# Issuing the copy of the first batch's p on VectorE in the order of its load's arrival, and telling the planner of it

## The chip, the cores and the metric

One core of a Trainium2 chip. The metric is device time of one execution in microseconds, the median of several runs. All inputs are in HBM at the start and the output is in HBM at the end.

## The reference, cut to what matters

```python
def sm_attn(qq, kk, vv):
    s = scale * np.matmul(qq, kk.transpose(0, 1, 3, 2))
    s = s - np.max(s, axis=-1, keepdims=True)
    a = np.exp(s)
    a = a / (np.sum(a, axis=-1, keepdims=True) + 1e-09)
    return np.matmul(a, vv)
p_packed = sm_attn(p, k, v)              # p: (8, 8, 32, 64), k, v, q: (8, 8, 576, 64)
out = sm_attn(q, p_packed, p_packed)
# then, with x = out as (4608, 512):
a = x @ w1; b = x @ w2                   # 512 x 1024
h = a * b @ w3                           # 1024 x 1024
return (h @ w_out)                       # 1024 x 512
```

Eight batches of an attention in two steps (32 rows of p "pack" each batch's keys and values, then q attends to the packed rows), followed by a gated feed-forward layer.

## The kernel before

The kernel multiplies w3 by w_out once, at the start (the "fold"), so that each batch needs one product fewer. For that, w3 has to be transposed on TensorE, chunk by chunk, each chunk copied out of PSUM, where TensorE's results stand (copied to tile w3T), and then multiplied. Everything that TensorE does is put in order at build time by a greedy planner: every piece of work is a `Step` with the things that it needs, times estimated for each engine, and a rule that the step that can start first goes first. Where the planner sees an idle stretch, it puts filler matmuls on a constant tile (`keep_busy`), to hold TensorE's clock up.

```python
def load_p(b0, b1):
    nc.gpsimd.dma_start(out=pin[:, 2*b0 : 2*b1, 0, :], in_=p[b0:b1].rearrange(...))
...
load_fold(0, 1)          # w3 columns and w_out rows of fold chunk 0
load_fold(1, 2)
...
load_fold(2, 4)
load_fold(4, 6)
load_in("k", 0)
load_p(0, 1)
load_in("v", 0)
load_fold(6, 8)
load_w3(4, 6)
load_in("q", 0)
load_gate(0, 2)
load_w3(6, 8)
load_gate(2, 4)
load_gate(4, 8)
load_p(1, B)
load_in("k", 1)
load_in("v", 1)
load_in("q", 1)
nc.vector.tensor_copy(pin[:, 0:2, 1, :], pin[:, 0:2, 0, :])   # batch 0's p, a second time beside itself
nc.gpsimd.tensor_copy(pin[:, 2:, 1, :], pin[:, 2:, 0, :])     # the other batches'
...   # only now the planner emits all the steps, among them:

def emit_p(e, tags):                     # in attention(b)
    ps = one(tags, FP16)
    for g in range(2):
        nc.tensor.transpose(ps[:, 128*g : 128*g + 128], pin[:, 2*b + g, :, :]..., ident[:, :])
    ...                                  # two copies out of PSUM to pT
turned("k", "kT")                        # four steps: transposes of k, copies to kT
front.append(Step(110, emit_p, needs=[("p", b), ("packed", b - 2)], ...))
s1(0); s1(1); s1(2)                      # scores and exp
front.append(Step(862, emit_pack, needs=[("v", b, 1)] + [("es1", b, i) for i in range(3)], ...))
```

An engine executes its instructions in the order in which they were emitted. So the copy of batch 0's p stands ahead of every copy of w3T on VectorE.

The softmax here doesn't subtract the row's maximum and nothing guards it: scores larger than these inputs give would overflow.

Of the kernel before, what the change touches and what calls it, by code (L numbers as in the profile page):

```python
# [17 lines left out]
def kernel(  # L18
# [12 lines left out]
    nc = tc.nc  # L31
# [3 lines left out]
    B, H, S, D = q.shape  # L35
# [56 lines left out]
    pin = wpool.tile([128, B * 2, 2, D], FP16, name="pin")  # L92
# [20 lines left out]
    def load_in(name, b, now=0.0):  # L113
        src = {"k": k, "v": v, "q": q}[name]
        t = in_pool.tile([128, H, CK * D], FP16, name=name, tag=name)
        ins[name, b] = t
        n = 1 if b else 2
        for i in range(n):
            h0, h1 = H * i // n, H * (i + 1) // n
            nc.gpsimd.dma_start(  # L120
                out=t[0:SC, h0:h1, :],
                in_=src[b, h0:h1].rearrange("h (p c) d -> p h (c d)", c=CK),
            )
            arrives((name, b, 1), (h1 - h0) * S * D * 4, now)
            if i == 0:
                done[name, b, 0] = done[name, b, 1]
# [59 lines left out]
    load_in("k", 1)  # L186
    load_in("v", 1)
    load_in("q", 1)
    nc.vector.tensor_copy(pin[:, 0:2, 1, :], pin[:, 0:2, 0, :])
    nc.gpsimd.tensor_copy(pin[:, 2:, 1, :], pin[:, 2:, 0, :])  # L190


    F0, F1, W0, W1 = 0.30, 0.90, 2.00, 9.00
    A0, A1, A2 = -2.00, -1.40, -0.20



# [106 lines left out]
    def one_bank(b):  # L304
        if b < EARLY:
            return lambda: [(x,) for x in SINGLE + ("m2",)]
        return lambda: [("m1",), ("m3",), ("m2",)]
# [9 lines left out]
    def one(tags, dtype=FP32):  # L317
        if tags[0] == "m2":
            n = 512 if dtype == FP32 else 1024
            return psum.tile([128, 2, n], dtype, name="m2", tag="m2")[:, 0, :]  # L320
        return bank(tags[0], dtype)

    def copy(e, out, in_):
        if e == "A":
            nc.scalar.copy(out=out, in_=in_)  # L325
        else:
            nc.vector.tensor_copy(out, in_)  # L327
# [3 lines left out]
    def attention(b):  # L331
        st = state[b] = {}
        front, back = [], []
# [20 lines left out]
        def turned(name, tname):  # L354

            for hp in range(NHP):

                def emit(e, tags, hp=hp):
                    if hp == 0:
                        st[tname] = t_pool.tile([128, NHP, S], FP16, name=tname, tag=tname)  # L360
                    ps = one(tags, FP16)
                    for hc in range(6):
                        h, c3 = 2 * hp + hc // 3, hc % 3
                        nc.tensor.transpose(  # L364
                            ps[:, SC * hc : SC * hc + SC],
                            ins[name, b][0:SC, h, 128 * c3 : 128 * c3 + 128],
                            ident[0:SC, 0:SC],
                        )
                    copy(e[0], st[tname][:, hp, :], ps[:, 0:S])
                    if hp == NHP - 1 and b + 2 < B:  # L370
                        load_in(name, b + 2, now["t"])

                needs = [(name, b, hp // 2)]
                if name == "q":
                    needs.append(("scored", b - 2))
                front.append(
                    Step(
                        255,
                        emit,
                        needs=needs,  # L380
                        tags=one_bank(b),
                        post=[({"D": 455, "A": 640}, (tname, b, hp), (0,))],
                    )
                )
# [172 lines left out]
        def norm_round(g):  # L557
# [16 lines left out]
            def emit_a2(e, tags):  # L574
# [20 lines left out]
            return Step(0, emit_a2, needs=[("ri", b, g)], post=[({"D": 458}, ("a2", b, g), ())])  # L595

        turned("k", "kT")
        front.append(
            Step(
                110,  # L600
                emit_p,
                needs=[("p", b), ("packed", b - 2)],
                tags=one_bank(b),
                post=[
                    ({"D": 250, "A": 370}, ("pT", b), ()),
                    ({"D": 250, "A": 370}, ("pT", b), (0,)),
                ],
# [9 lines left out]
                needs=[("v", b, 1)] + [("es1", b, i) for i in range(3)],  # L617
                tags=one_bank(b),
                post=[({"D": 640}, ("ppn", b), (0,))],
# [4 lines left out]
        if b != 1:  # L624
# [5 lines left out]
                needs=[("ppn", b), ("grounds", b - 2)],  # L630
                tags=one_bank(b),
                post=[({"D": 260, "A": 380}, ("ppT", b), (0,))],
# [244 lines left out]
    for key in ("gated", "scored", "grounds", "packed"):  # L877
        done[key, -2] = done[key, -1] = 0.0
    att = [attention(b) for b in range(B)]
    work = [s for pair in range(B // 2) for s in project(pair)]  # L880
    run(
# [37 lines left out]
```

## Time and profile before

| | before |
|---|---|
| median of 3 runs | 237.88 us (237.17 to 238.91) |
| TensorE busy | 211.8 of 235.8 us |
| VectorE, ScalarE busy | 122.0, 139.4 us |
| TensorE's longest wait | 9.2 us, for a copy on VectorE |

In the profile, PE is TensorE's matmuls, PEld its weight loads, DVE VectorE, ACT ScalarE, POOL GpSimd. `out<-in` gives the tiles. What stands behind `<-` in brackets is what ended the idle time before the instruction, and the number before it is how long that lasted. The lines are in the prediction below.

### The profile page before, as it was taken

The page shows a single profiled execution, that of the slowest core. Times are in us where ns is not written, and L with a number is a line of the kernel's source. Part 1 is how long each engine was busy: PE and PEld are TensorE (multiplying, and loading weights), DVE is VectorE, ACT ScalarE, POOL GpSimd, SP SyncE. Part 2 cuts the span into 40 slices and gives each one's busy share as a digit, 9 for nine tenths or more (in the row PEclk, how much of TensorE's full clock was granted, in tenths as well). Part 3 has the DMA queues.
Part 4 walks back from the last instruction along what each step waited for, and adds up shares of the span by engine and source line. Part 5 has one row for each costly group of instructions (what it writes and reads, how often), then busy time and mean ns, then how long its engine had stood idle before and what let it go on. Part 6 is the DMA issues. An engine that isn't in the chain of part 4 may idle for free.

```text
span 235.8 us, 6617 instructions
## 1 busy us (share of the span) xinstructions
PE 211.8 (90%) x2736; PEld 130.6 (55%) x2767; DVE 122.0 (52%) x286; ACT 139.4 (59%) x291; POOL 36.6 (16%) x54
## 2 busy tenths in 40 slices
PE   7409899999799999998999899999999999999992
PEld 2104555457665668575666466646765545566540
DVE  1002316456572858886865594574766476444300
ACT  2000326767488688767768578776865676555421
POOL 8856440501121202111111000000000000000000
PEclk9967979999999999999999999999999999999999
DMA  7999999999999997959839422122123222332364
GB/s 78 144 198 206 198 204 198 196 204 205 170 155 186 189 201 103 197 92 170 132 81 165 83 72 47 47 72 65 46 49 90 47 79 57 89 75 65 87 156 112
DMA packets 34190, 29.52 MB, mean 125 GB/s; under 512 B 4976, under 2 KB 29040, under 8 KB 34160
## 3 DMA queue, kind: packets, MB, share of 16 engines
q0 software_dynamic: 28400, 19.66, 58.2%
q1 hardware_dynamic: 5760, 9.44, 15.3%
q8 instruction: 21, 0.34, 0.6%
q14 instruction: 9, 0.07, 0.1%
HBM read 39.32 MB, written 9.44 MB: 207 GB/s over the span
## 4 chain that ended last, share of the span: by engine, by line
PE 79%; DMA 8%; issue 3%; ACT 3%; DVE 3%; POOL 3%; DVEq 0%; ACTq 0%; POOLq 0%
PE g L673 27%; PE f L737 19%; PE m L364 7%; PE m L737 4%; DMA q<-in_q_dram 4%; PE m L483 4%; PE g L737 4%; DMA k<-in_k_dram 3%; PE m L396 3%; PE m L432 3%; DVE abT L684 2%; POOL w_sb L129 1%; PE m L797 1%; PE g L831 1%; PE m L519 1%
## 5 line engine op out<-in xcount | busy, mean ns | idle before, releaser
L673 PE MATMUL g<-a,G 128*128 128x288 f16 x512 | 87.7, 286 | 3.2 <-DVE abT L684 2.8
L684 DVE TENSOR_TENSOR abT<-g,bs 128x288 bf16<-128x288 f32 x128 | 57.7, 455 | 51.5 <-PE g L673 22.7
L673 PEld LDWEIGHTS <-G 128*128 128x128 f16 x512 | 46.2, 98 | 35.2 <-issue 11.5
L325 ACT CAST bs<-g 128x288 bf16<-128x288 f32 x128 | 50.1, 402 | 25.9 <-PE g L673 22.9
L737 PE MATMUL f<-wc_sb,abT 128*128 128x512 bf16 x186 | 55.7, 379 | 2.0 <-ACT o L325 0.3
L737 PEld LDWEIGHTS <-abT 128*128 128x128 bf16 x288 | 27.0, 98 | 15.5 <-issue 2.9
L327 DVE CAST G<-m 128x512 f16<-128x512 f32 (+1 forms) x32 | 20.1, 669 | 4.3 <-PE m L483 4.2
L325 ACT CAST G<-m 128x1024 f16<-128x1024 f32 (+1 forms) x17 | 16.4, 962 | 9.5 <-PE m L483 9.5
L325 ACT COPY kT<-m 128x576 f16<-128x576 f16 x8 | 5.2, 644 | 26.3 <-PE m L364 26.0
L737 PE MATMUL m<-wc_sb,abT 128*128 128x512 bf16 x47 | 13.4, 379 | 0.1
L403 ACT ACTIVATE es<-m 96x512 f16<-96x512 f32 x24 | 12.8, 596 | 1.1 <-PE m L396 1.1
L325 ACT COPY o<-f 128x512 f32<-128x512 f32 x18 | 10.6, 588 | 4.1 <-PE f L737 3.4
L364 PE MATMUL m<-ident,q 96*128 96x96 f16 x174 | 11.6, 206 | 1.5 <-issue 1.4
L364 PEld LDWEIGHTS <-q 96*128 96x128 f16 x192 | 10.5, 97 | 3.8 <-issue 2.0
L120 POOL DMA_DIRECT2D v<-in_v_dram x9 | 6.8, 760 | 37.1 <-PE m L432 36.4
L396 PEld LDWEIGHTS <-kT 128*96 128x96 f16 x192 | 10.6, 125 | 2.7 <-DVE pT L327 0.9
L831 PE MATMUL f<-wo_sb,w3T 128*128 128x512 f16 x8 | 3.7, 468 | 9.2 <-DVE w3T L327 9.2
L364 PE MATMUL m<-ident,k 96*128 96x96 f16 x192 | 11.7, 206 | 0.1
L364 PEld LDWEIGHTS <-k 96*128 96x128 f16 x192 | 10.4, 97 | 2.4 <-issue 0.3
L327 DVE COPY kT<-m 128x576 f16<-128x576 f16 x24 | 10.7, 451 | 1.6 <-PE m L364 1.1
L396 PE MATMUL m<-pT,kT 128*96 128x64 f16 x192 | 10.6, 208 | 1.0 <-DVE pT L327 0.7
L241 PE MATMUL m<-blk 128*128 128x512 f16 x26 | 10.0, 519 | 1.5 <-DVE blk L167 1.5
(76 smaller groups left out, 223.0 us busy)
## 6 DMA issues: line engine op xcount, KB each, us to landing
out_dram<-o SPq DMA_DIRECT2D x24, 192.0 KB, 2.4
k<-in_k_dram POOLq DMA_DIRECT2D x7, 576.0 KB, 8.8
v<-in_v_dram POOLq DMA_DIRECT2D x7, 576.0 KB, 6.7
q<-in_q_dram POOLq DMA_DIRECT2D x7, 576.0 KB, 8.5
out_dram<-o SPq DMA_DIRECT2D x24, 128.0 KB, 2.4
w_sb<-in_moe_w_dram POOLq DMA_DIRECT2D x4, 512.0 KB, 13.4
w_sb<-in_moe_w_dram POOLq DMA_DIRECT2D x7, 256.0 KB, 11.6
out_dram<-o SPq DMA_DIRECT2D x24, 64.0 KB, 2.0
```

Of the source, the lines that this page charges most:

```text
L120: nc.gpsimd.dma_start(out=t[0:SC, h0:h1, :], in_=src[b, h0:h1].rearrange("h (p c) d -> p h (c d)", c=CK),)
L241: nc.tensor.matmul(ps[:, :], blk[:, :], blk[:, :].unsqueeze(1).to_broadcast([128, 4, 128]), start=True, stop=True,)
L325: nc.scalar.copy(out=out, in_=in_)
L327: nc.vector.tensor_copy(out, in_)
L364: nc.tensor.transpose(ps[:, SC * hc : SC * hc + SC], ins[name, b][0:SC, h, 128 * c3 : 128 * c3 + 128], ident[0:SC, 0:SC],)
L396: nc.tensor.matmul(o[:, :, h % 2, h // 2, :], st["kT"][:, h // 2, c : c + SC], pT[:, h, :, :], start=True, stop=True,)
L403: nc.scalar.activation(out=st["es1"][0:SC, c3, :, :, :, :].rearrange("t e g h n -> t (e g h n)"), in_=ps[0:SC, :], func=AF.Exp, scale=scale,)
L432: nc.tensor.matmul(ps[32 * hp : 32 * hp + 32, 128 * g + d0 : 128 * g + d1], es1[0:SC, c // 2, c % 2, g, hp, :], vin[0:SC, 2 * hp + g, D * ...
L483: nc.tensor.matmul(banks[g][32 * hp : 32 * hp + 32, 0:n], ppT[64 * g : 64 * g + 64, g, 32 * hp : 32 * hp + 32], w_sb[w][64 * g : 64 * g + ...
L673: nc.tensor.matmul(ps[:, 0:HS], st["G", w][:, g, 128 * mc : 128 * mc + 128], st["a2"][:, g, half, :], start=(g == 0), stop=(g == 1),)
L684: nc.vector.tensor_mul(abT[b // 2][:, mc, b % 2, HS * half : HS * half + HS], ps[:, 0:HS], st["bs"][:, :],)
L737: nc.tensor.matmul(hold["ps"][:, :], lhsT(i), rhs(i), start=(i == 0), stop=(i == n - 1))
```

## The change

The intent: issue the copy of batch 0's p in the order in which its data arrives, so that VectorE can copy w3T chunks out of PSUM from the first microseconds. The planner is told of it, as a step of its own.

```diff
     load_in("q", 1)
-    nc.vector.tensor_copy(pin[:, 0:2, 1, :], pin[:, 0:2, 0, :])
     nc.gpsimd.tensor_copy(pin[:, 2:, 1, :], pin[:, 2:, 0, :])
 
-    F0, F1, W0, W1 = 0.30, 0.90, 2.00, 9.00
-    A0, A1, A2 = -2.00, -1.40, -0.20
+    F0, F1, W0, W1 = 0.3, 0.9, 2.0, B + 1
+    A0, A1, A2 = -2, -1.4, -0.2
 ...
         turned("k", "kT")
+        if b == 0:
+
+            def emit_pin(e, tags):
+                nc.vector.tensor_copy(pin[:, 0:2, 1, :], pin[:, 0:2, 0, :])
+
+            front.append(
+                Step(0, emit_pin, needs=[("p", 0)], post=[({"D": 200}, ("pin", 0), ())])
+            )
         front.append(
             Step(
                 110,
                 emit_p,
-                needs=[("p", b), ("packed", b - 2)],
+                needs=[("pin" if b == 0 else "p", b), ("packed", b - 2)],
```

## The prediction

> **What bounds the kernel now.** I began with the page's busy slices (each digit is the busy share of 5.9 us).
>
> ```profile
> PE   7409899999799999998999899999999999999992
> DVE  1002316456572858886865594574766476444300
> PEclk9967979999999999999999999999999999999999
> DMA  7999999999999997959839422122123222332364
> ```
>
> TensorE is busy 90% of the span; from the fourth slice on it is almost full to the end. The only hole is in slices two and three (about 6 to 18 us). The DMA row is full through it, so a hole in the start could simply be the loads. The list of waits, restricted to 0 to 45 us, says otherwise for TensorE:
>
> ```profile
> DVE pin L189 <- DMA pin<-in_p_dram: 15.1, 1, 15.1
> PE f L831 <- DVE w3T L327: 9.2, 1, 9.2
> ```
>
> TensorE stood 9.2 us once, for VectorE's copy of a transposed w3 chunk; VectorE stood 15.1 us for the load of p. The timelines of TensorE and VectorE (start, length, what) join the two:
>
> ```profile
> 6.97 0.38 PE L797 MATMUL m<-ident,w_sb 128*128 128x128 f16 x4
> 8.28 0.38 PE L797 MATMUL m<-ident,w_sb 128*128 128x128 f16 x4
> 17.86 0.61 PE L831 MATMUL f<-wo_sb,w3T 128*128 128x512 f16 x1 [9.20 <-DVE w3T L327]
> ...
> 17.27 0.20 DVE L189 COPY pin<-pin 128x128 f16<-128x128 f16 x1 [15.13 <-DMA pin<-in_p_dram]
> 17.38 0.75 DVE L327 COPY w3T<-m 128x512 f16<-128x512 f16 x2
> ```
>
> The first w3 chunk was transposed at 6.97 to 7.35 us, the second by 8.66. Their copies out of PSUM need only VectorE, but the copy of p was issued ahead of them, and p lands at 17.3. So both copies run at 17.4, and the fold matmuls that need them start at 17.86. One 0.20 us instruction at the head of a queue costs TensorE 9.2 us.
>
> Two checks. First, w3's and w_out's first chunks (w3 passes through the tile named w_sb in the trace) landed after 3.0 to 4.5 us from issues at 1.3 to 3.4, by 7.9 at the latest; the fold was not short of data. Second, the chain that ended last names a load of q from 15.87 to 25.92. I don't follow it there: what starts at 25.92 is the transposes of k. Their two issues, at 7.43 and 8.14, landed after 8.1 and 8.9 us, at 15.6 and 17.0. In the weight-load timeline TensorE works from 17.85 to 25.92 with no gap above 0.35 us: k waited for its turn behind five fold chunks.
>
> After 48 us only small waits are left on TensorE (2.8 us in all for abT, in 8 pieces). So a shift of TensorE's stream at the start should reach the end, unless a load stops it.
>
> **What the Trainium skill says.** "PSUM — Partial Sum Buffer", section "Engine vs sequencer instructions": VectorE's queue is strictly first in, first out, and matmuls start and finish in program order. The trace agrees: two ready copies stood behind the copy of p until 17.3, and k, landed at 17.0, stood behind the fold until 25.9. "TensorE: Matmul & The Clock Gate", section "What's actually happening": the array falls to half clock after an idle window of about 3.4 us and regains full clock after as much busy time. The trace agrees in kind: after the 9.2 us hole the granted clock reads 0.65 in 12 to 18 us and 0.78 in 18 to 24, and 128x512 fold matmuls last up to 634 ns against 379. It matters here because the hole is also paid for in slow matmuls after it.
>
> **The change part by part.**
>
> Constants: 0.30 to 0.3, 9.00 to B + 1 with B = 8, and so on: the same values, cost nothing.
>
> Removed: the early VectorE copy of p (0.20 us, and the 15.1 us in front of it). The GpSimd copy of the other seven batches stays; it runs at 44.21 as before.
>
> Added: the same copy as a step of batch 0's stream, after its four k transposes and before the transposes of p. It then stands behind the k copies on VectorE, about 0.2 us on the way from p to the scores. The planner that fixes the order at build time now knows of the copy, with 200 ns on VectorE. I had the kernel before print its plan and followed the new step through it by hand, for order alone: the copy goes behind the third k copy, which delays p's transposes in the plan by some 0.7 us, and may let the transpose of w3 chunk 6 go ahead of the packing of batch 0. The plan meets again at the load of q, which it waits for in either case. So I take the order as unchanged afterwards, with small differences possible.
>
> Moved: chunk 0's copy goes from 17.4 to about 7.5, its fold matmuls from 17.86 to about 8.7, right behind chunk 1's transposes. Upper limit of the shift: 17.86 - 8.66 = 9.2 us.
>
> What limits the shift is the loads. They are issued by GpSimd, whose queue at the start is held by earlier DMAs and not by the fold, so I let them land when they land now. In the views by tile, the issue time and the time to landing are, as line (last figure the longest):
>
> ```profile
> L120 POOL DMA_DIRECT2D k<-in_k_dram x3: 703/713/781, 7.4 to 29.8; - x3
> DMA to landing us min/median/max: 8.1/8.9/17.4
> L106 POOL DMA_DIRECT2D pin<-in_p_dram x2: 745/915/1085, 8.8 to 28.5; - x2
> DMA to landing us min/median/max: 8.5/12.1/15.7
> ```
>
> For k: the issue at 29.8 with 17.4 us lands batch 1's k at 47.2. In the same way, one issue at a time, and beside it when TensorE starts on it now, with the room between:
>
> - k of batch 0, second half: lands 17.0, its transposes at about 26.6, room 9.6
> - v of batch 0: 10.2 + 10.0 = 20.2, used 29.5, room 9.3
> - w3 columns 6 and 7: 11.7 + 9.7 = 21.4, used 31.25, room 9.9
> - w3 rows 4 and 5: 14.4 + 10.9 = 25.3, used 35.74, room 10.4
> - q of batch 0, both halves: 26.8 and 28.2, used 37.07 and 38.87, room 10.3
> - w3 rows 6 and 7: 20.5 + 13.2 = 33.7, used 43.32, room 9.6
> - gate weights, last part: 27.0 + 14.6 = 41.6, used 51.18, room 9.6
> - **k of batch 1**: 47.2, used 54.61, **room 7.4**
> - v of batch 1: 31.2 + 18.7 = 49.9, used 59.80, room 9.9
> - q of batch 1: 34.0 + 18.3 = 52.3, used 61.67, room 9.4
> - k of batch 2: 45.1 + 10.1 = 55.2, used 64.53, room 9.3
>
> The rows used for this, of TensorE's timeline:
>
> ```profile
> 25.92 1.38 PE L364 MATMUL m<-ident,k 96*128 96x96 f16 x24
> 37.07 0.41 PE L364 MATMUL m<-ident,q 96*128 96x96 f16 x6
> 54.61 0.93 PE L364 MATMUL m<-ident,k 96*128 96x96 f16 x18
> ```
>
> From batch 3 on, the loads are issued when TensorE has finished with a buffer, so they move with it; k of batch 3 (issued 56.4, landing 63.9, used 77.9) has 14 us of room.
>
> All rooms but one are above the 9.2 us that TensorE can move. The exception holds it to 7.4: by then it would arrive some 1.8 us early at batch 1's k and wait. Those 1.8 us also soak up small losses before that point (the 0.2 us of the copy on the path, 0.3 us behind the w3 transpose in front of the packing, a few matmuls at low clock while TensorE waits between loads). So the sum: 9.2 - 1.8 = 7.4 us, and I take off 0.1 for what is not soaked up: 237.9 - 7.3 = 230.6 us, 3% less.
>
> **The rivals.**
>
> *The loads take the place of the wait.* If TensorE at the start were bound by DMA anyway, chunks would run earlier and then wait at k or q, and little would be won. For it: DMA is full until about 90 us. Against it: every room in the list but one is above 9 us, so the data has been lying there. A weaker form is likely, and is in my sum as the 1.8 us at k. If loads slip by another 2 us, because VectorE and TensorE now work beside GpSimd's issuing, the gain is about 5 us: 233.
>
> *The whole 9.2 us arrive at the end.* If k of batch 1 lands a little earlier than I read, or TensorE's wait there overlaps waits that exist now (1.2 us at 62 us, for nothing that the profile shows), the time would go to 229.
>
> *VectorE or ScalarE becomes the bound, or the order gets worse.* Both are busy below 60% (DVE 52%, ACT 59%), and the change adds no work to them. The planner is greedy, so a different moment for one copy may reorder ties later; I give this 1 us either way. A slower clock is a part of it: the waits between loads are shorter than the hole now, but there are more of them, and the fold chunks after batch 0's packing run slowly today (630 ns at 31.7 to 34 us). One or two more slow microseconds there would still be covered by the wait for k.
>
> *Nothing happens*: the copy was hidden. The 9.2 us on TensorE, its busiest engine, speak against it.
>
> **Range and chances.** Middle 230.6. Full shift: 229; loads two or more microseconds late, or an unlucky order: 233. I give 228.9 to 232.9 eight chances in ten. The 2% line is at 237.9 x 0.98 = 233.1, a gain of 4.8 us. That the gain falls short of it needs loads later by over 2.5 us or a reordering that costs as much: 0.11 for within 2%, 0.01 for slower, 0.88 for faster.
>
> **What the changed profile would show.** VectorE's first w3T copy at about 7.5 us, without the copy of p ahead of it; the wait of 9.2 us gone, and in its place several waits on TensorE of 0.3 to 1.5 us for loads between 9 and 21 us; k of batch 0 transposed at 15.6 to 17.7; q of batch 0 at about 28.5 instead of 37.07; a wait of 1 to 2 us in front of batch 1's k at 47.2; from there on the old picture, about 7.4 us early. The prediction is wrong if the loads land later than now, if TensorE reaches k of batch 1 later than 47.2 by more than a microsecond, or if the shift at 60 us isn't the shift at the end.

## The result, and the profile after

| | before | after |
|---|---|---|
| median | 238.39 us (4 runs) | 231.22 us (4 runs, 230.64 to 231.67) |
| span of the profiled run | 235.8 us | 229.4 us |
| ratio of the fast runs | | 0.9715, 95% interval 0.9663 to 0.9766 |

A ratio here is the mean time of one kernel's fast runs over that of the other's in the same rounds, so it is not quite the ratio of the two medians. One run of the kernel before (241.57 us) was more than 1.5% above the fastest, so slow, and is left out of the ratio; the others were fast. The changed kernel is faster by 2.9%, inside the predicted range of 228.9 to 232.9.

The busy slices of the changed kernel:

```profile
PE   7776999997999989999997999999999999999992
DVE  1231243564818668767673864666586376444300
PEclk9998599999999999999999999999999999999999
```

The two empty slices of TensorE are gone; VectorE works from the second slice on. The clock shows one dip, in the fourth and fifth slices, where the kernel before had two, in the third and fourth and in the sixth. VectorE's first copies, from its timeline:

```profile
6.25 0.42 DVE L326 COPY w3T<-m 128x512 f16<-128x512 f16 x1 [4.12 <-PE m L804]
7.55 0.42 DVE L326 COPY w3T<-m 128x512 f16<-128x512 f16 x1 [0.88 <-PE m L804]
...
18.39 0.18 DVE L600 COPY pin<-pin 128x128 f16<-128x128 f16 x1
```

The w3T copies now wait for nothing but TensorE's transposes, and the copy of p runs at 18.39 without a wait of its own. What TensorE does with the time, from its timeline:

```profile
7.35 0.38 PE L838 MATMUL f<-wo_sb,w3T 128*128 128x512 f16 x1
...
10.05 0.40 PE L804 MATMUL m<-ident,w_sb 128*128 128x128 f16 x4 [1.02 <-DMA w_sb<-in_moe_w_dram]
...
17.55 0.69 PE L363 MATMUL m<-ident,k 96*128 96x96 f16 x12 [0.75 <-DMA k<-in_k_dram]
...
22.04 0.61 PE L804 MATMUL m<-ident,w_sb 128*128 128x128 f16 x4 [1.04 <-DMA w_sb<-in_moe_w_dram]
...
30.06 0.41 PE L363 MATMUL m<-ident,q 96*128 96x96 f16 x6
...
47.59 0.93 PE L363 MATMUL m<-ident,k 96*128 96x96 f16 x18
...
56.28 0.50 PE L363 MATMUL m<-ident,q 96*128 96x96 f16 x8 [1.29 <-issue]
...
84.40 0.24 PE L363 MATMUL m<-ident,q 96*128 96x96 f16 x2 [0.53 <-issue]
```

The fold begins at 7.35 instead of 17.86. In place of one wait of 9.2 us there are several of about 1 us for loads. The second line with w_sb shows the new order: the transposes of w3 chunk 6 now stand ahead of batch 0's packing. Batch 1's k is transposed at 47.59 instead of 54.61, **7.0 us sooner**, with no wait for its load on TensorE's matmuls; the load was issued at 31.36 and took 16.0 us, so it landed at 47.4. The last two lines are stops for nothing that the profile names; they matter below.

How far a kernel is ahead of the one before can be followed at fixed places of the program: the packing of batches 1 to 4 (59.80, 73.92, 88.11 and 101.77 us before), and the last group of ten matmuls of the final projection (222.12 before). In the changed kernel the lead is 7.0, 6.9, 7.1, 6.4 and 6.4 us. The lead is 7.0 us already at the transposes of batch 0's q (30.06 for 37.07). So it is won by 30 us and kept, but for 0.7 us lost between batch 3 and batch 4, where the 0.53 us stop at 84.40 stands.

### The profile page after: what moved, and what is told of

It reads as the page before. It is cut to its first block, busy times and chain, and to the rows that moved or that the text cites. A ratio compares the mean times of both kernels' runs of the same rounds, so it can differ in the third digit from the quotient of the medians.

```text
span 229.4 us, 6620 instructions
## 1 busy us (share of the span) xinstructions
PE 211.2 (92%) x2738; PEld 130.2 (57%) x2769; DVE 121.1 (53%) x285; ACT 139.6 (61%) x292; POOL 36.6 (16%) x54
## 4 chain that ended last, share of the span: by engine, by line
PE 81%; DMA 7%; issue 3%; ACT 3%; DVE 2%; POOL 2%; DVEq 0%; ACTq 0%; POOLq 0%
PE g L680 28%; PE f L744 20%; PE m L363 7%; PE m L744 4%; DMA w_sb<-in_moe_w_dram 4%; PE m L482 4%; PE g L744 4%; PE m L395 3%; PE m L431 3%; DMA wo_sb<-in_moe_w_out_dram 3%; DVE abT L691 2%; PE g L838 1%; PE m L804 1%; PE m L518 1%; PE m L560 1%
## 5 line engine op out<-in xcount | busy, mean ns | idle before, releaser
L326 DVE COPY w3T<-m 128x512 f16<-128x512 f16 (+1 forms) x11 | 5.5, 497 | 20.3 <-PE m L804 20.3
L324 ACT COPY kT<-m 128x576 f16<-128x576 f16 x8 | 5.1, 644 | 17.3 <-PE m L363 17.0
L363 PEld LDWEIGHTS <-k 96*128 96x128 f16 x192 | 10.2, 97 | 3.4 <-DMA k<-in_k_dram 1.7
L570 ACT ACTIVATE ri<-ln 128x576 f16<-128x576 f32 x16 | 10.9, 683 | 0.5
```

Source lines behind the costliest of these rows:

```text
L324: nc.scalar.copy(out=out, in_=in_)
L326: nc.vector.tensor_copy(out, in_)
L363: nc.tensor.transpose(ps[:, SC * hc : SC * hc + SC], ins[name, b][0:SC, h, 128 * c3 : 128 * c3 + 128], ident[0:SC, 0:SC],)
L570: nc.scalar.activation(out=ri[:, :, :], in_=ln[:, :, :], func=AF.Exp, scale=-1.0)
```

## The experiments

Theory A: the copy at the head of VectorE's in-order queue cost TensorE 9.2 us; the gain is that wait, less what the loads take back. Rival: the gain comes from the planner, which knows of the copy now and orders TensorE's work differently. The first group tells these apart.

| run | median, us | ratio to before, fast runs, 95% interval |
|---|---|---|
| e1_scalare_copy | 230.85 (6 runs) | 0.9698 (0.9651 to 0.9745) |
| e2_plan_only | 239.74 (4 runs) | 1.0005 (0.9923 to 1.0086) |
| e3_queue_only | 230.98 (6 runs) | 0.9690 (0.9650 to 0.9730) |
| e4_p_loaded_sooner | 232.23 (6 runs) | 0.9741 (0.9699 to 0.9784) |
| e5_k1_sooner | 231.48 (6 runs) | 0.9713 (0.9677 to 0.9749) |
| e6_filled_gaps | 230.84 (6 runs) | 0.9692 (0.9657 to 0.9727) |
| e7_k1_and_filled | 230.84 (5 runs) | 0.9690 (0.9655 to 0.9725) |
| e8_changed_again | 231.19 (6 runs) | 0.9703 (0.9666 to 0.9741) |
| e9_both_narrow | 230.99 (6 runs) | 0.9706 (0.9666 to 0.9746) |
| e10_filled_narrow | 231.46 (6 runs) | 0.9730 (0.9687 to 0.9774) |

The first four shared a chip and 11 runs of the kernel before (median 238.36); the next four another (238.04), the last two a third (237.59, one run of the kernel before there was slow, as was one of e2, 243.05 us; both are left out of the ratios, but not of the medians; e2's fast runs have a median of 239.50). All results were correct.

### e1_scalare_copy: the same copy, on another engine's queue

```diff
-    nc.vector.tensor_copy(pin[:, 0:2, 1, :], pin[:, 0:2, 0, :])
+    nc.scalar.copy(out=pin[:, 0:2, 1, :], in_=pin[:, 0:2, 0, :])
```

> The kernel before with the one copy of batch 0's p given to ScalarE at the same place in the program; TensorE's instructions and their order are those of before, the planner knows of nothing. Theory (the 9.2 us come from the copy standing at the head of VectorE's queue): ScalarE has nothing to do until k arrives at 16, so its wait for p at 17.3 costs nothing or little (its first k copy may slip by up to 1 us); the first w3T copy on VectorE runs at 6 to 8 us, and the time falls to 230 to 232 us, like the changed kernel. Rival (the gain comes from the planner, which now knows of the copy and fills the gap behind it): no gain, 237 to 239 us.

230.85 us. The timeline of ScalarE shows that the wait is still there, only where it does no harm:

```profile
18.14 0.30 ACT L189 COPY pin<-pin 128x128 f16<-128x128 f16 x1 [16.11 <-DMA pin<-in_p_dram]
```

ScalarE waits 16.1 us for p, longer than VectorE did, and the kernel is as fast as the changed one. TensorE's instructions and their order are those of before. It isn't the wait that costs, but whose queue it heads.

### e2_plan_only: the new plan, with the copy at its old place

```diff
+    nc.vector.tensor_copy(pin[:, 0:2, 1, :], pin[:, 0:2, 0, :])
     nc.gpsimd.tensor_copy(pin[:, 2:, 1, :], pin[:, 2:, 0, :])
...
             def emit_pin(e, tags):
-                nc.vector.tensor_copy(pin[:, 0:2, 1, :], pin[:, 0:2, 0, :])
+                pass
```

> The changed kernel with the copy of p back at its early place: TensorE, ScalarE and GpSimd have exactly the changed kernel's instructions in the changed kernel's order, only VectorE has the copy ahead of the w3T copies again. Theory (head of the queue): the wait of about 9 us on TensorE is back and the time is 237 to 239 us. Rival (the new order of TensorE's work is what helps): 231 to 234 us.

239.74 us, no gain. The list of waits has the old one again:

```profile
PE f L839 <- DVE w3T L327: 10.2, 1, 10.2
```

p landed at 18.2 in this run, hence 10.2 us and not 9.2. The planner's part of the change is worth nothing by itself, within the 0.9% of the interval.

### e3_queue_only: the copy moved, the planner not told

```diff
-    nc.vector.tensor_copy(pin[:, 0:2, 1, :], pin[:, 0:2, 0, :])
...
         def emit_p(e, tags):
+            if b == 0:
+                nc.vector.tensor_copy(pin[:, 0:2, 1, :], pin[:, 0:2, 0, :])
             ps = one(tags, FP16)
```

> The kernel before with the copy of p issued just ahead of the transposes of p, and the planner not told of it: TensorE's order is exactly that of before, so the packing of batch 0 stands ahead of the transposes of w3 chunk 6 again. Theory (the queue alone): 230 to 232 us. If the changed order (w3 chunk 6 ahead of the packing, two filler matmuls more) cost the changed kernel something, this one is faster than it by 0.3 to 1 us; if TensorE then meets the load of batch 1's k (landing at about 47.4), the two are the same within 0.3 us, and a wait for k shows on TensorE.

230.98 us: moving one line has the whole gain. TensorE's timeline, at the transposes of k of batches 0 and 1:

```profile
18.97 0.29 PE L343 MATMUL m<-ident,pin 128*128 128x128 f16 x2 [0.40 <-DVE pin L340]
...
48.01 0.94 PE L365 MATMUL m<-ident,k 96*128 96x96 f16 x18 [0.97 <-DMA k<-in_k_dram]
```

The copy on the path from p to the scores costs TensorE 0.40 us, which the changed kernel fills with two filler matmuls. Here the wait for batch 1's k that the prediction forecast is seen, 0.97 us. In the changed kernel it isn't. Two things differ there: TensorE comes later by itself, as its w3 chunk 6, ahead of the packing, waited 1.04 us for its load (2.54 us in the second profile, e8), and k landed at 47.4 us, in e3 at 48.0. The two kernels take the same time, within what the runs can tell.

### e4_p_loaded_sooner: a smaller dose

```diff
     load_fold(2, 4)
+    load_p(0, 1)
     load_fold(4, 6)
     load_in("k", 0)
-    load_p(0, 1)
```

> The kernel before with nothing changed but the place of p's load in GpSimd's queue: two loads earlier, behind the weights of fold chunks 2 and 3. TensorE, VectorE and ScalarE keep their instructions and order, so the copy of p still heads VectorE's queue. p should land at about 11.8 us instead of 17.3. Theory (the wait for p sets when TensorE's stream starts, and the shift reaches the end one for one as long as it is below 7 us): the first fold matmul at about 12.4 instead of 17.9, and the time 5 to 6 us less than before, 232 to 233.5 us. Rival (TensorE's start isn't what counts, the loads of batch 1 are): no change, or the whole gain of the changed kernel.

232.23 us. All instructions of TensorE, VectorE and ScalarE are those of before, in the same order. VectorE's and TensorE's timelines:

```profile
11.78 0.20 DVE L189 COPY pin<-pin 128x128 f16<-128x128 f16 x1 [9.64 <-DMA pin<-in_p_dram]
...
12.36 0.61 PE L831 MATMUL f<-wo_sb,w3T 128*128 128x512 f16 x1 [3.56 <-DVE w3T L327]
```

The fold starts 5.5 us sooner (12.36 for 17.86), and the lead is 5.4 us at batch 1's packing and 5.8 at the end. A shift of this size goes through to the end one for one. Theory A stands; the rival has fallen with e2 and e3.

What remains is the size. TensorE could have moved by 9.2 us, and the lead is 7. The prediction's sum gave that to one thing, the load of batch 1's k. A second group, built on e3_queue_only, tests it against another loss that the profile after shows, the clock. The view of TensorE by stretches, in the changed kernel (start and end, length, busy time and count of each engine, then granted clock, DMA share and GB/s):

```profile
18.00:21.00 3.00, 2.16 (x34) 1.55 (x31) 0.84 (x3) 1.69 (x4) 2.00 (x4) 1.00 1.36 200
21.00:22.50 1.50, 0.46 (x4) 0.34 (x4) 0.00 (x0) 0.88 (x2) 0.88 (x2) 0.65 1.26 212
22.50:28.00 5.50, 5.50 (x112) 2.94 (x111) 1.44 (x4) 0.00 (x0) 2.50 (x4) 0.50 1.24 205
```

From about 21.4 to 28.3 us TensorE runs at half clock, through the fold matmuls of chunks 5 to 7. This isn't a loss that the change brought: the kernel before was granted half clock from 13.8 to 20.6 us and from 30.8 to 34.2, and worked for 6.1 us of that time; the changed kernel worked for 6.2 us at half clock. What is new are waits. The same view from the start to batch 1's k, before and after:

```profile
0.00:54.61 54.61, 42.11 (x424) 22.02 (x426) 17.01 (x44) 18.12 (x34) 25.06 (x39) 0.91 1.25 181
0.00:47.59 47.59, 41.20 (x426) 21.57 (x428) 16.11 (x43) 18.46 (x35) 24.64 (x39) 0.93 1.24 177
```

TensorE's matmuls are idle for 12.5 us before (54.61 less 42.11) and for 6.4 after, 6.1 less. So of the 9.2 us that went, 3.1 came back as other idle time, for w3 (2.1 us) and k of batch 0 (0.75) above all; 0.9 us less of busy time makes up the 7.0 us.

### e5_k1_sooner: the load of batch 1's k taken forward

```diff
-    load_p(1, B)
+    load_p(1, 2)
     load_in("k", 1)
     load_in("v", 1)
     load_in("q", 1)
+    load_p(2, B)
...          # cut to the order of the loads; the code that hands the planner the old times is left out
```

The GpSimd copy is split likewise, its second part issued at batch 1. The planner is given the old times, so no engine but GpSimd has another order.

> The kernel of the run with the copy moved and the planner untold (231.0 us, a wait of 0.97 us for batch 1's k at 47 us), with the load of p for batches 2 to 7 taken out from in front of k, v and q of batch 1 and put behind them; the planner is told the old times, so that all engines but GpSimd keep their order. k of batch 1 should land some 2 us sooner, at about 45.5. Theory (the load of k is one of two limits, and TensorE's own stream arrives there only 0.2 to 1 us before it): the wait is gone and the time falls by 0.2 to 0.9 us, no more. Rival (k's load alone caps the shift at 7.4 us, as the prediction's sum has it): it falls by 1.5 us or more, towards 229.

231.48 us, no gain that the runs can tell; the expected 0.2 to 0.9 us didn't come, and the rival's 1.5 us didn't either. In its profile k lands at 44.9 (issued 30.5, 14.4 us) and is transposed without a wait, 8.2 us ahead of the kernel before:

```profile
46.37 0.93 PE L378 MATMUL m<-ident,k 96*128 96x96 f16 x18
```

So the wait was removed, and the lead at batch 1's packing is 8.2 us, but by batch 4 it is 6.9.

### e6_filled_gaps: dummy work in TensorE's short waits

```diff
+                    if b == 0 and name == "k" and hp == 2:
+                        warm_t(ps, 12)          # 12 transposes of the constant tile into the step's own PSUM tile
...          # in emit_p for b == 0: warm_t(ps, 6); in s1 for b == c3 == 0: warm_m(ps, 3)
...          # in emit_pack for b == 0: warm_m(ps, 3), matmuls of 128x512
```

> The same base, with TensorE's idle gaps between 17 and 22 us filled by dummy work that lengthens nothing: 12 transposes ahead of the third k group, 6 ahead of those of p, 3 matmuls of 128x512 ahead of the first scores, 3 ahead of the packing. Theory (the gaps are what puts the clock to half for 6.8 us, from 20 to 27): the half-clock window disappears or shrinks to 3.4 us, q of batch 0 is transposed 1 to 2 us sooner than at 29.6, but TensorE then waits longer for batch 1's k, so the time falls by 0.3 us at most. Rival (the clock is not a matter of these gaps): the granted clock stays at half for 6.8 us, the time is the same or up to 0.5 us more.

230.84 us. The same stretches as above, in this kernel:

```profile
18.00:21.00 3.00, 2.90 (x42) 2.07 (x40) 1.14 (x4) 1.49 (x3) 2.00 (x4) 1.00 1.36 202
21.00:22.50 1.50, 1.46 (x86) 0.89 (x85) 0.00 (x0) 0.72 (x2) 0.65 (x1) 1.00 1.26 209
22.50:28.00 5.50, 5.08 (x60) 3.05 (x60) 3.00 (x6) 2.38 (x4) 2.43 (x4) 1.00 1.25 203
```

The half-clock stretch is gone, entirely, and in all six runs: their mean granted clocks are 0.996 to 1.00, those of e3 0.978 to 0.993. And q of batch 0 is transposed at 27.58 instead of 29.55 in e3. Of these 2.0 us, 0.35 were there already at batch 0's k (16.09 for 16.44), so the slow clock had cost about 1.6 us. TensorE's timeline at batch 1's k, and after it:

```profile
46.88 0.94 PE L383 MATMUL m<-ident,k 96*128 96x96 f16 x18 [1.20 <-DMA k<-in_k_dram]
...
54.01 0.23 PE L455 MATMUL m<-ones,es 96*32 96x1 f16 x10 [1.09 <-issue]
```

TensorE waits for k again, 1.20 us (0.97 in e3), and passes it 1.1 us sooner than in e3 as k landed at 46.8 here and at 48.0 there. As expected, the time hardly moves.

### e7_k1_and_filled: both

The two edits together.

> Both of the former together. Theory (two limits in series, the half clock and the load of k): the gain is more than the sum of the two, 1 to 2 us below the base, 229 to 230 us, with the loads of q's second half and of the last gate weights as the next waits. Rival (TensorE's stream is set by the loads before q in any case): within 0.5 us of the run with k sooner alone.

230.84 us: **expected was 229 to 230, and this failed.** The first half of the expectation came true. TensorE's timeline:

```profile
45.46 0.93 PE L396 MATMUL m<-ident,k 96*128 96x96 f16 x18
...
53.33 0.23 PE L468 MATMUL m<-ones,es 96*32 96x1 f16 x10 [1.84 <-issue]
```

k of batch 1 is transposed at 45.46, 9.15 us before the old 54.61. So with the half clock and the wait for k both gone, nothing holds TensorE back to 7 us at that place. This is as long as the hole was, but not the hole alone: the 6.1 us of work at half clock are gone too, and other waits are in. But then TensorE stops for 1.84 us in the middle of batch 1's packing, its clock drops to half for 3.4 us, and at batch 2's packing the lead is 7.0 us again.

### e8_changed_again: the changed kernel as reference

> The changed kernel unaltered, as the reference of this group on the same chip: 230.5 to 231.5 us, and the same waits as in its first profile; where its half-clock stretch falls may differ[...]. If its k of batch 1 is again reached within 0.3 us of its landing, that balance belongs to the change; if a wait of about 1 us shows, it is chance.

231.19 us. The balance at k was chance to a degree: here k landed at 47.2 and TensorE came at 48.04, 0.9 us later, after a wait of 2.54 us of w3 chunk 6.

```profile
23.18 0.61 PE L804 MATMUL m<-ident,w_sb 128*128 128x128 f16 x4 [2.54 <-DMA w_sb<-in_moe_w_dram]
...
48.04 0.93 PE L363 MATMUL m<-ident,k 96*128 96x96 f16 x18
```

### The stops without a name

Every profile has stops of TensorE that it puts down to "issue", time in which it waited for nothing that the profile shows. In the program's order of TensorE's instructions, counted from its start, they stand here (from the timelines, matched with the program's order):

| kernel | what stands there | instruction | stop, us |
|---|---|---|---|
| before | q of batch 1; q of batch 2 | 1212; 1724 | 1.18; 0.27 |
| after | q of batch 1; q of batch 3 | 1212; 2236 | 1.29; 0.53 |
| e6 | packing of batch 1; q of batch 2 | 1212; 1724 | 1.09; 0.85 |
| e7 | packing of batch 1; gate matmul behind packing of batch 4 | 1212; 2748 | 1.84; 0.41 |

The place goes by count: 48 dummy instructions more in e6 and e7 move the stop to other work, and it stays at 1212. All are 1212 plus a multiple of 256. The same holds in all 12 traces, for all 22 such stops of TensorE's matmuls above 0.2 us (the records counted are 1 to 9 short of it, as some are missing from a trace). The Trainium skill's page "Runtime: NRT & Kernel Launch", section "Instruction fetch mechanics", says that instructions are refilled in blocks of 16 KiB, 256 instructions. The trace agrees: its DMA queue marked as instruction has 21 packets of 0.34 MB in all, 16 KB each, for about 5,540 instructions of TensorE.

```profile
q8 instruction: 21, 0.34, 0.6%
```

The packed traces also hold the time of each of these packets. In the changed kernel, packets are under way from 53.88 to 54.98 us and from 81.96 to 82.86; the stops end at 56.28 and 84.40. In the 12 traces all 22 stops end 1.30 to 1.73 us after the last such packet landed, which reads as: a stop ends when its block of instructions has come. There is one packet for each border. Those for borders up to 84 us in the changed kernel start 1.7 to 3.7 us after TensorE passed the border before; of the 12 later ones all but one start at most 1.1 us after. DMA is over 90% busy until about 92 us.

The last group writes each planned filler matmul as four narrow ones, on e7 and e6:

```diff
-        for _ in range(n):
+        for i in range(4 * n):
             nc.tensor.matmul(
-                ps[:, :], blk[:, :], blk[:, :].unsqueeze(1).to_broadcast([128, 4, 128]),
+                ps[:, 128 * (i % 4) : 128 * (i % 4) + 128], blk[:, :], blk[:, :],
```

> The kernel with k of batch 1 sooner and the gaps filled (230.8 us), with each filler matmul of 128x512 that the planner places written as four of 128x128: the same filler work, 216 TensorE instructions more ahead of batch 1. In all traces so far TensorE stood 0.8 to 2 us with nothing to wait for at its record 1215 to 1217, whatever stood there (q transposes, or the middle of batch 1's packing). Theory (a limit by count of instructions: TensorE runs out of fetched instructions at a fixed place of its program): the stop is again at record 1215 to 1220 although that is now a gate matmul ahead of batch 1's packing, and the next one 512 further on; as fewer tiny matmuls stand before it, it is shorter than 2.0 us, and the time falls by 0.3 to 1 us, to 229.8 to 230.5. Rival (the stop belongs to the packing and what follows it, a wait that the profile does not name): it stays in or right behind batch 1's packing, now record 1256 to 1446, and the time is the same.

> The kernel with the gaps filled and k of batch 1 at its old place (230.8 us), with the same narrow fillers. The wait of 1.2 us for k of batch 1 stays, in front of the stop at record 1215 to 1220. Theory (count of instructions): the stop is at the same record as in the other run of this group, shorter than 1.1 us because TensorE has just waited for k while instructions could be fetched, and the time is 230 to 231. Rival (a wait of the packing): the stop is behind the packing, 1 us or more.

230.99 and 231.46 us, no gain. Neither expectation held as written: e9's gain didn't come, e10 is 0.5 us above its range. The stop isn't at 1212 but at 1468, which is 1212 + 256, and what stands there is again q of batch 1, behind the packing, as the rival had it. The later two, at 1980 and 2492, stand behind no packing and on the count. e9's timeline:

```profile
45.37 0.93 PE L396 MATMUL m<-ident,k 96*128 96x96 f16 x18
...
54.31 0.29 PE L396 MATMUL m<-ident,q 96*128 96x96 f16 x3 [0.83 <-issue]
...
70.30 0.81 PE L396 MATMUL m<-ident,k 96*128 96x96 f16 x15 [0.40 <-issue]
...
85.57 0.30 PE L709 MATMUL g<-a,G 128*128 128x288 f16 x1 [1.57 <-issue]
```

So a border doesn't always bring a stop (1212 brings none here), and it doesn't take a burst of tiny instructions just before it: a packing has 192 in about 1 us, but in the 3 us before the stops at 70.30 and 85.57 there are 58 and 84. Nor does a burst suffice: in the kernel before, a border at 150.4 us has 182 instructions in the last microsecond and no stop. The stop is shorter than in e7, 0.83 us, and the lead is 9.2 us at batch 1's packing and 8.2 at batch 2's; but two more stops follow, and by batch 4 the lead is 6.1 us. That the missing instructions are the reason is read from the count and from the packets' times; no run changed the fetching alone. Why the packets come late is open. That they start later while the loads fill the DMA speaks for a contention with these, but no run tests it.

## Why the prediction was right, point by point

- **Head of the queue.** Right, and shown: the wait on another engine's queue costs nothing (e1), the old place brings it back (e2), moving the line alone has the gain (e3), and a shorter wait (3.56 us left of 9.20) gives the matching part (e4).
- **Shift of TensorE's start, 9.2 us at most.** Right for the hole. The fold began at 7.35 us, sooner than the 8.7 forecast; in this execution the full clock was granted from 4.4 us on, in e8 from 7.5, and there the fold began at 8.75. The changed kernel reached 7.0 us at batch 1's k; e7 and e9 reach 9.15 and 9.2, but without the half clock, which the kernel before has.
- **Loads land when they land now.** Nearly: in the changed kernel the second half of batch 0's k landed at 17.5 (17.0 before), p at 17.7 (17.3), the second half of batch 0's q at 29.95 (28.18), the last gate weights at 42.7 (41.7), batch 1's k at 47.4 (47.2), its q at 53.1 (52.3). So loads slipped by 0.2 to 1.8 us, the one that the sum rests on by 0.2. (One reading is off: the second issue of batch 0's k starts at 8.11, not 8.14.)
- **Room of 7.4 us at batch 1's k, so a loss of 1.8 us by a wait there.** The size of the loss was nearly right (2.2 us), its mechanism wrong for the changed kernel, and that the two numbers meet is luck. The lead was 7.0 us already at batch 0's q, at 30 us; then TensorE arrived just as k landed, or 0.9 us after (e8), and no wait of 1 to 2 us stands there. What failed is the size of the small losses before that point: the prediction named some 0.5 us and a few slow matmuls, and let the 1.8 us soak them up. Measured were 3.1 us of other idle time up to k, less 0.9 us of busy time. The half clock, which a rival of the prediction names, stayed as long as before, for 6.2 us of work against 6.1; e6 shows that it costs about 1.6 us. The forecast wait appears elsewhere, at 0.97 us in e3, 1.20 in e6 and 1.14 in e10. The two limits lie within about a microsecond of each other, and removing either gains nothing (e5, e6).
- **q of batch 0 at about 28.5.** Wrong: 30.06, for the same reason. Without the half clock it is 27.58 (e6).
- **Order of the plan.** Right: w3 chunk 6 went ahead of the packing, two filler matmuls more, and after that TensorE's order is the old one but for the place of two fold matmuls and one filler. Three copies out of PSUM changed between VectorE and ScalarE.
- **The shift at 60 us is the shift at the end.** Nearly: 7.0 and 6.4 us in the profiled run, 6.6 and 6.5 in e8. The prediction mentioned the 1.2 us at 62 us "for nothing that the profile shows" and let it rest; it belonged to a family of stops, which stand where the leads of e7 and e9 fall from 9.2 us to 7 and less. Of the prediction's three signs of being wrong, later loads came true, by little for the one that it rests on; TensorE was at k 0.4 and 0.8 us (e8) after 47.2, within its microsecond.

A version that beats the changed kernel was not found. e1, e3, e6, e7 and e9 lie 0.2 to 0.4 us below it by medians, inside the noise; e3_queue_only is the simplest of them.

## What to carry to other kernels

On an in-order engine, an instruction that waits for a load belongs behind everything that is ready sooner; look for it with the list of waits, by following the longest wait of the busiest engine one link further, to what its releaser was itself waiting for. Before counting on the whole hole, list for each load when it lands and when it is used now: the smallest room bounds the gain. Then size the waits that come in place of the hole as carefully, since here they took the 2 us before the smallest room could (7.4 us forecast, 7.0 measured, by luck). When two or three limits lie close together, single experiments on each will all say "no effect"; follow the lead at fixed places of the program instead of the total time.

## What the Trainium skill lacked or had wrong

- "Runtime: NRT & Kernel Launch", section "Instruction fetch mechanics", says that crossing a block border is mostly hidden, as instructions are issued more slowly than they are fetched. Here TensorE stopped at borders of 256 instructions for 0.27 to 1.84 us, and went on 1.30 to 1.73 us after the packet had landed. That a stop can take 1.8 us and is listed as "issue" isn't said.
- "TensorE: Matmul & The Clock Gate", section "What's actually happening", ties the half clock to an idle window of about 3.4 us. Less idleness was enough here: in the 3.4 us before the clock fell at 21.44 us in the changed kernel, TensorE was busy for 2.1 us, with waits of 0.77 us and of 1.04 us (not yet over); before the fall at 30.82 us in the kernel before, busy for 2.2 us, with none above 0.68. Filling the gaps (2.90 of 3.00 us busy) removed 6.8 us of half clock. The same page does say, in its section "A second HAM failure mode: psum-queue depth-cycling", that frequent short idling throws the clock back, but gives no length of gaps. Whether busy share in a window is what counts isn't shown.
- The first-in, first-out queues of "PSUM — Partial Sum Buffer", section "Engine vs sequencer instructions", held in all runs; that a 0.20 us instruction can thereby cost another engine 9.2 us is no page's example.
